# A cosine-attention and MLP kernel: the first 18 pairs of heads in another written order

## The chip, the cores and the metric

The kernel runs on one core of a Trainium2 chip. The metric is the time of one execution on the device in microseconds; for the kernel before it is the median of 3 runs. The profile comes from one further execution, which has a time of its own. The core's engines work side by side, each through its own queue in the order in which the program gives it instructions: TensorE (PE, with its weight loads shown as PEld), VectorE (DVE), ScalarE (ACT), GpSimd (POOL), and SyncE (SP), which here only starts DMAs. An instruction that waits holds up all that stands behind it in its engine's queue.

## The reference

Attention with normalised queries and keys, then an MLP on its output:

```
q_n = q / (norm(q) + 1e-6);  k_n = k / (norm(k) + 1e-6)
attn = softmax(q_n @ k_n^T / tau)          # 8 batches x 12 heads, 448 x 64, tau = 0.1
x = (attn @ v), put to 3584 x 768
h = x @ w_in                               # 768 -> 2048
g = h * clip(h + 3, 0, 6) / 6
out = g @ w_out                            # 2048 -> 768, 3584 rows
```

Inputs and output are 32-bit floats; the matrix products run in 16-bit floats.

## The kernel before

The 96 heads are 48 pairs (8 batches times 6). A pair i goes through these steps, whose names are used from here on; j is an item, a q or a k of two pairs, and a step's last letter says on which engine it runs (a is ACT, v DVE, p POOL):

- LQ.j loads a q or k item (448 KB, L197) and LV loads v (four DMAs, L211), both on SP's queue.
- SQ squares an item (L226 on ACT, L228 on DVE or POOL; some items in parts), RE sums the rows (DVE, L240), NO (or NA and ND) makes the reciprocal norms on ACT (L256 to L259), NM normalises (L296).
- TR transposes an item on PE (seven matmuls, L342); XD does it by a transposing DMA on SP (L353). CQ, CK and CS copy the result to where the scores read it: `kz` for k, `tT` for q, `km` for a rest (L362 on ACT, L364 and L392 on DVE, L402 on POOL).
- SC.i.c makes the scores of one of four parts of a pair (PE, L442 and L445), EX.i.c their exponentials on ACT (L464).
- VC casts v (L313 on DVE, L315 on POOL and ACT), VA.i.c multiplies by v on PE into PV (L487), FI divides by the row sums (DVE, L507 and L508).
- BK transposes the result on PE (L525, L527), or XP and XB by DMA (L559, L546); CX copies it into `xT`, the MLP's input.

The MLP runs in units U on PE, taken from a list in fixed order: one 128-wide slice of the first matmul (L609, called F0.0 to F0.15 for batch 0 and F1.x for batch 1), a tile of the second matmul (L682, S0), or one of the products of a scheme that multiplies 2 x 2 blocks with fewer products (L818, named 3.-1, 4.-1 and so on). UA and UV do what a unit leaves to ACT and to DVE: the relu (L629) and the product u times M that goes to `gT` (L636), or the store of a tile. UP does sums on POOL.

The scheme needs sums of blocks of `w_out`: WS.x.e.h makes half h of sum x on engine e (L762, 128 x 1536 elements). 6, 7 and 1 go to `w_sum`; y3 and y4 go back into `w_out_sb` itself. Sums of blocks of `gT` are GS (L796) and GL. W starts the next of ten loads of weights on POOL's queue (L1036; six pieces of `w_in`, then four of `w_out`).

D.n and DP.n issue n matmuls on zeros, of 512 and of 248 columns (L1043, L1048), which go nowhere: they keep PE busy while it would wait. PSUM has two score banks and the banks Y and Z until OPEN; from then on scores and units take their banks from a ring of six (M0, M1, Y, Z, M2, M3), so that a bank comes round when its readers (EX, or UA and UV) are done.

What sets the order: pairs 0 to 17 (`FIRST = 18`) follow PLAN, 38 strings of such names, written out by hand. The program goes through it from left to right and gives each engine its instructions in that sequence, so two neighbours on one engine keep their order, and two on different engines are bound only by data, buffers and banks. Each step asserts that the steps it needs stand ahead of it. Pairs 18 to 47 are issued by a loop, which is the same in both kernels. PLAN's interpreter:

```
def run(text):
    for t in text.split():
        op, *args = t.split(".")
        do(op, *(int(a) if a.lstrip("-").isdigit() else a for a in args))

for line in PLAN:
    run(line)
```

Of the kernel before, what the change touches and what calls it, by code (L numbers as in the profile page):

```python
# [18 lines left out]
ORDER = "1111111111111111111111111111112222222122"  # L19

PLAN = [
# [38 lines left out]
]  # L60


# [1164 lines left out]
```

## Time and profile before

| | us |
|---|---|
| time, median of 3 runs (lowest, highest) | 401.3 (401.23, 401.36) |
| the profiled execution | 401.5 |
| its span in the profile | 399.7 |
| PE busy | 391.1 |
| DVE busy | 291.4 |
| ACT busy | 274.1 |
| POOL busy | 235.7 |

The span runs from the first to the last instruction that the profile shows. Busy times of different engines lie side by side in it. PLAN's part ends some 120 us into the span; until 58 us there is too little for PE to do without attention, and until about 8 us the first items are on their way.

In a row of the timeline the first number is the start, the second the length, both in us, then the engine, the line, the operation, what it writes and reads, and the count of like instructions in a row; in square brackets stands the idle time ahead of it and what ended that. In a row of waits stand engine and line, what was waited for, the sum, the times, and the longest. Rows by window list busy time and count for each engine, then the granted clock (1.00 is full), the share of the DMA engines and what they moved in GB/s.

### The profile page before, as it was taken

How to read it: one execution, taken by the hardware profiler on the slowest of the kernel's cores; microseconds unless marked ns; L12 is line 12 of the kernel's file. 1: busy time of each engine (PE TensorE's matmuls, PEld its weight loads, DVE VectorE, ACT ScalarE, POOL GpSimd, SP SyncE). 2: the span in 40 equal slices, each digit the busy share in tenths (PEclk: the TensorE clock that was granted, in tenths of full speed). 3: DMA queues.
4: the chain of work that ended last, by engine and by line, in shares of the span. 5: the costliest groups of instructions: out<-in, count | busy, mean ns of one | idle time of the engine just before them, and what ended most of it. 6: DMA issues, size and time to landing. Idle time of an engine off the chain costs nothing.

```text
span 399.7 us, 9624 instructions
## 1 busy us (share of the span) xinstructions
PE 391.1 (98%) x3669; PEld 231.3 (58%) x3669; DVE 291.4 (73%) x514; ACT 274.1 (69%) x627; POOL 235.7 (59%) x234
## 2 busy tenths in 40 slices
PE   7999999999999999999999999999999999999996
PEld 5666466555565555555555555555565556555563
DVE  7797987889788688767888775976756565645663
ACT  6999999777887676887776776767658655224230
POOL 6896628552574989579769839788395500500070
PEclk9999999999999999999999999999999999999999
DMA  8999995896997778795879296884843424130123
GB/s 290 278 267 234 240 274 158 149 200 138 232 180 161 180 177 179 164 231 157 196 171 241 78 202 158 174 184 135 194 111 88 103 48 67 45 75 21 30 71 97
DMA packets 92365, 63.73 MB, mean 159 GB/s; under 512 B 56096, under 2 KB 91552, under 8 KB 92320
## 3 DMA queue, kind: packets, MB, share of 16 engines
q1 hardware_dynamic: 87408, 56.45, 58.0%
q0 software_dynamic: 4512, 6.29, 9.2%
q8 instruction: 28, 0.46, 0.5%
q10 hardware_dynamic: 400, 0.39, 0.3%
q14 instruction: 17, 0.14, 0.1%
HBM read 45.61 MB, written 11.01 MB: 142 GB/s over the span
## 4 chain that ended last, share of the span: by engine, by line
PE 92%; ACT 5%; DVE 2%; issue 0%; ACTq 0%
PE M L609 25%; PE M L818 20%; PE PV L487 11%; PE Y L609 6%; PE Z L609 6%; PE M L445 6%; PE Z L818 5%; PE Y L818 4%; ACT at L464 4%; PE PV L1048 2%; PE Y L445 1%; PE M L906 1%; PE Z L445 1%; DVE w_out_sb L762 1%; PE M L682 1%; PE Z L682 1%
## 5 line engine op out<-in xcount | busy, mean ns | idle before, releaser
L609 PE MATMUL M<-xT,w_in_sb 128*128 128x448 bf16 x516 | 109.4, 352 | 0.1
L609 PEld LDWEIGHTS <-w_in_sb 128*128 128x128 bf16 x768 | 72.1, 98 | 62.3 <-issue 1.8
L464 ACT ACTIVATE at<-M 128x448 bf16<-128x448 f32 x194 | 96.9, 568 | 14.6 <-PE M L445 13.6
L296 POOL TENSOR_TENSOR nrm<-big,nr 128x896 bf16<-128x896 f32 (+1 forms) x45 | 76.4, 1700 | 26.2 <-ACT nr L259 15.7
L228 POOL TENSOR_TENSOR big<-big 128x896 f32<-128x896 f32 (+3 forms) x41 | 62.0, 1517 | 15.5 <-DVE n L240 10.2
L636 DVE SCALAR_TENSOR_TENSOR gT<-u,M 128x448 bf16<-128x448 bf16 x75 | 45.4, 616 | 31.6 <-ACT u L629 31.2
L629 ACT ACTIVATE u<-M 128x448 bf16<-128x448 f32 x86 | 48.0, 561 | 28.4 <-PE M L609 27.0
L487 PEld LDWEIGHTS <-at 128*128 128x128 bf16 (+1 forms) x1536 | 53.5, 97 | 22.2 <-issue 13.4
L487 PE MATMUL PV<-vx,at 128*128 128x65 bf16 (+1 forms) x1536 | 62.4, 193 | 0.1
L240 DVE TENSOR_REDUCE n<-big 128x14 f32<-128x896 f32 (+1 forms) x50 | 51.6, 1041 | 5.8 <-POOL big L228 2.9
L818 PEld LDWEIGHTS <-gT 128*128 128x128 bf16 x336 | 32.5, 98 | 24.6 <-issue 1.7
L847 POOL TENSOR_TENSOR big<-big 128x384 f32<-128x384 f32 x13 | 13.5, 1035 | 53.6 <-ACT big L871 53.5
L818 PE MATMUL M<-w_out_sb,gT 128*128 128x384 bf16 x224 | 40.3, 326 | 0.9 <-DVE w_out_sb L762 0.9
L818 PEld LDWEIGHTS <-gs 128*128 128x128 bf16 x280 | 27.0, 98 | 18.5 <-issue 0.4
L402 POOL COPY km<-tT 64x128 bf16<-64x128 bf16 x34 | 12.9, 379 | 38.7 <-PE M L445 13.8
L508 DVE TENSOR_TENSOR on<-PV,rc 128x512 bf16<-128x512 f32 x48 | 33.2, 691 | 1.7
L818 PE MATMUL M<-w_sum,gs 128*128 128x384 bf16 (+1 forms) x192 | 34.2, 323 | 0.0
L464 ACT ACTIVATE at<-Y 128x448 bf16<-128x448 f32 x51 | 28.9, 566 | 6.0 <-PE Z L445 5.9
L445 PE MATMUL M<-tT,kz 64*128 64x448 bf16 (+1 forms) x171 | 31.9, 350 | 0.1
L609 PE MATMUL Y<-xT,w_in_sb 128*128 128x448 bf16 x132 | 28.7, 353 | 0.0
L464 ACT ACTIVATE at<-Z 128x448 bf16<-128x448 f32 x49 | 27.8, 568 | 0.8 <-PE M L445 0.8
L315 POOL CAST vx<-big 128x512 bf16<-128x512 f32 x37 | 24.5, 665 | 3.7 <-PE PV L487 3.3
(138 smaller groups left out, 564.8 us busy)
## 6 DMA issues: line engine op xcount, KB each, us to landing
big<-in_k_dram SPq DMA_DIRECT2D x24, 448.0 KB, 4.6
big<-in_q_dram SPq DMA_DIRECT2D x24, 448.0 KB, 4.2
out_dram<-o SPq DMA_DIRECT2D x107, 96.0 KB, 2.2
big<-in_v_dram SPq DMA_DIRECT2D x48, 128.0 KB, 3.9
big<-in_v_dram SPq DMA_DIRECT2D x48, 96.0 KB, 3.8
w_out_sb<-in_moe_w_out_dram POOLq DMA_DIRECT2D x4, 768.0 KB, 9.1
w_in_sb<-in_moe_w_in_dram POOLq DMA_DIRECT2D x4, 384.0 KB, 8.9
w_in_sb<-in_moe_w_in_dram POOLq DMA_DIRECT2D x2, 768.0 KB, 15.1
```

The source lines that it names most:

```text
L228: engines[e].tensor_tensor(out=o, in0=i, in1=i, op=ALU.mult)
L240: nc.vector.tensor_reduce(out=n2s[d % 2][:, j % 2, c], in_=sq[:, :, :, :].rearrange("p g c d -> p (g c) d")[:, c, :], axis=AX.X, op=ALU.add,)
L296: engines[e].tensor_tensor(out=nrm[:, :, g, :].rearrange("p c g d -> p g c d"), in0=raw_of[j][:, g, :, :], in1=rs[d % 2][3][:, j % 2, :] . ...
L315: (engines[e].copy if e == "a" else engines[e].tensor_copy)(out=o, in_=f)
L445: nc.tensor.matmul(o, ks, qt[rows], start=True, stop=True)
L464: nc.scalar.activation(out=o, in_=x, func=AF.Exp, scale=inv_tau)
L487: nc.tensor.matmul(pv_out(j, h), at[rows, n, q_cols(i // HP, j)], vt[rows, 3 + h if name == "M" else 5 * h + int(name[1]), :], start=(name ...
L508: nc.vector.tensor_tensor(out=on[:, :, :, :].rearrange("p j h d -> p h j d"), in0=pv4[:, :, :, 0:D], in1=rc[:, :, :].to_broadcast([128, 2, ...
L609: nc.tensor.matmul(ps[:, 0:S], w_in_sb[:, cc, fc * 128 : (fc + 1) * 128], x[:, cc, 0:S], start=(cc == 0), stop=(cc == CC - 1),)
L629: nc.scalar.activation(out=u[:, :], in_=ps[:, 0:S], func=AF.Relu, bias=0.5, scale=1.0 / 6.0)
L636: nc.vector.scalar_tensor_tensor(out=g[:, fc, c0 : c0 + S], in0=u[:, :], scalar=1.0, in1=ps[:, 0:S], op0=ALU.min, op1=ALU.mult,)
L818: nc.tensor.matmul(m, lhs[:, c, :], rhs[:, c, c0 : c0 + width], start=(base is None and c == 0), stop=(c == KC - 1), skip_group_check=True,)
```

## The change

Only the 38 strings of PLAN differ. The steps are the same but for the engine of seven and the count of dummies: CK.0, CS.6, CS.9 and CX.9 go from DVE to ACT, CQ.13 from ACT to DVE, VC.11 from POOL to DVE, VC.19 from ACT to POOL; the short dummies (DP) go from 75 to 64. All else is order. The second and third rows of PLAN, as an example:

```diff
-    "NO.0.1 LQ.5 LQ.4 LV.0 DP.5 DP.8 DP.1 DP.2 SQ.3.a.0.7 NM.1.p.0 DP.6 DP.4 D.10 SQ.0.v.6.2 RE.0.0 RE.0.1 DP.4",
-    "NM.1.v.1 NO.0.0 NM.0.p.0 SQ.2.a.0.7 RE.3 RE.2 NM.0.p.1 TR.1.Y TR.0.Z CK.0.v DP.4 SQ.4.p.0.7 CQ.0.v LQ.6",
+    "NO.0.1 LQ.5 LQ.4 LQ.6 LV.0 DP.8 DP.5 SQ.3.a.0.7 SQ.0.v.6.2 RE.0.0 RE.0.1 NM.1.v.1 NM.1.p.0 DP.4 D.10 NO.0.0",
+    "NM.0.p.0 SQ.2.a.0.7 RE.3 SQ.5.a.0.7 RE.2 NM.0.p.1 TR.1.Y SQ.4.p.0.7 DP.4 DP.2 TR.0.Z CQ.0.v CK.0.a DP.4 DP.1",
...
```

On PE the first transposes (TR.1, TR.0) stood behind 30 short, 10 long and 4 short dummies; now behind 21 short and 10 long, with 6 short ones between the two. ACT's queue at this place, before (L226 squares, L256 to L259 norms, L464 the first exps; `tT` here is the copy CQ.1):

```order
L226 ACTIVATE big<-big 128x896 x2
L256 ACTIVATE ln_106<-n_103 128x28
L257 ACTIVATE nr_107<-ln_106 128x28
L258 ACTIVATE ln_106<-nr_107 128x28
L259 ACTIVATE nr_107<-ln_106 128x28
L362 COPY tT_84<-Z 128x448
L464 ACTIVATE at_0_86<-SC_149 128x2x448
```

and now:

```order
L226 ACTIVATE big<-big 128x896 x2
L362 COPY kz_80<-Y 128x448
L256 ACTIVATE ln_106<-n_103 128x28
L257 ACTIVATE nr_107<-ln_106 128x28
L258 ACTIVATE ln_106<-nr_107 128x28
L259 ACTIVATE nr_107<-ln_106 128x28
L362 COPY tT_84<-Z 128x448
L464 ACTIVATE at_0_86<-SC_149 128x2x448
```

The copy of the first transposed k (CK.0) came in ahead of the four norm steps of the second pair of items.

DVE's queue at the weight sums, before (the first L762 is WS.y3.v.0, then WS.6.v.1, FI.13 in two rows, WS.1.v.1, WS.7.v.1, a copy that stores a tile, and three at once: y3.v.1, y4.v.0, y4.v.1; L392 is CK.15 at the top and CK.16 at the end):

```order
L392 COPY kz1_81<-tT0_83 128x384
L636 SCALAR_TENSOR_TENSOR gT1_72<-u_1594,M1_649 128x448
L762 TENSOR_TENSOR w_out_sb_68<-w_out_sb_68 128x4x384
L762 TENSOR_TENSOR w_sum6_74<-w_out_sb_68 128x1536
L507 RECIPROCAL rc_1660<-PV_109 128x8
L508 TENSOR_TENSOR on_1535<-PV_109,rc_1660 128x2x4x64
L762 TENSOR_TENSOR w_sum1_73<-w_out_sb_68 128x1536
L762 TENSOR_TENSOR w_sum7_75<-w_out_sb_68 128x1536
L695 COPY o_1666<-Z_111 128x384
L762 TENSOR_TENSOR w_out_sb_68<-w_out_sb_68 128x4x384 x3
L392 COPY kz0_80<-tT0_83 128x384
```

and now (from the last product of F1, L636):

```order
L636 SCALAR_TENSOR_TENSOR gT1_72<-u_1582,M1_667 128x448
L762 TENSOR_TENSOR w_sum7_75<-w_out_sb_68 128x1536
L762 TENSOR_TENSOR w_sum6_74<-w_out_sb_68 128x1536
L762 TENSOR_TENSOR w_out_sb_68<-w_out_sb_68 128x4x384
L507 RECIPROCAL rc_1647<-PV_109 128x8
L508 TENSOR_TENSOR on_1521<-PV_109,rc_1647 128x2x4x64
L392 COPY kz1_81<-tT0_83 128x384
L762 TENSOR_TENSOR w_sum1_73<-w_out_sb_68 128x1536
L695 COPY o_1672<-Z_111 128x384
L762 TENSOR_TENSOR w_out_sb_68<-w_out_sb_68 128x4x384 x3
L313 TENSOR_REDUCE vx1_96<-big_94 128x8x64
L392 COPY kz0_80<-tT0_83 128x384
```

CK.15 went behind three pieces and FI.13; SP's transposing DMA XD.16 follows it in PLAN and needs its buffer, and POOL's NM.19 in turn waits for XD.16. WS.7.v.1 went to the front, and the cast VC.17 (L313) came in ahead of CK.16. Farther up, WS.6.v.0 now stands ahead of the product (UV) of F1.8 instead of behind it and CK.14, and on POOL WS.1.p.0 ahead of CS.14.

SP's queue around the loads of items 13 to 18, before (the k load at the top is LQ.14; L211 rows are LV.5; the five after them LQ.13, 15, 18, 17, 16; L559 is XP.6):

```order
L197 DMA big_94<-in_k_dram 128x2x448
L211 DMA big_94<-in_v_dram 64x2x256
L211 DMA big_94<-in_v_dram 64x2x192 x2
L211 DMA big_94<-in_v_dram 64x2x256
L197 DMA big_94<-in_k_dram 128x2x448
L197 DMA big_94<-in_q_dram 128x2x448
L197 DMA big_94<-in_k_dram 128x2x448
L197 DMA big_94<-in_q_dram 128x2x448
L197 DMA big_94<-in_k_dram 128x2x448
L559 DMA_TRANSPOSE xT1_70<-on_871 128x8x128
```

and now:

```order
L211 DMA big_94<-in_v_dram 64x2x192 x2
L211 DMA big_94<-in_v_dram 64x2x256
L197 DMA big_94<-in_k_dram 128x2x448
L197 DMA big_94<-in_q_dram 128x2x448
L197 DMA big_94<-in_k_dram 128x2x448 x3
L197 DMA big_94<-in_q_dram 128x2x448
L559 DMA_TRANSPOSE xT1_70<-on_865 128x8x128
```

LQ.14 went from ahead of LV.5 to behind LQ.18: the order is now LQ.13, 15, 18, 14, 16, 17.

72 rows, old and new, of the table PLAN are left out of this document.

## The prediction

> **What bounds the kernel now.** I read the page's head first, then the waits of the matmul engine, then busy time by stage, and only then the places where the rows of PLAN differ.
>
> ```profile
> span 399.7 us, 9624 instructions
> PE 391.1 (98%) x3669; PEld 231.3 (58%) x3669; DVE 291.4 (73%) x514; ACT 274.1 (69%) x627; POOL 235.7 (59%) x234
> PE 92%; ACT 5%; DVE 2%; issue 0%; ACTq 0%
> ```
>
> PE is busy for 98% of the span and the chain that ended last runs on it for 92%. What an edit of the order can win is therefore PE's idle time, PE's own filler work, and the 5% in which the chain runs on ACT. Over the whole span PE waits at four places:
>
> ```profile
> PE PV L1048 <- DVE vx L1099: 2.5, 1, 2.5
> PE M L818 <- DVE w_out_sb L762: 0.9, 1, 0.9
> PE SC L445 <- ACT at L464: 0.3, 1, 0.3
> PE SC L442 <- ACT at L464: 0.2, 1, 0.2
> ```
>
> The first, 2.5 us, is the wait for the memsets ahead of PLAN, which do not change. The second is one stall in the weight sums. Busy time by stage (us; busy time and count of PE, PEld, DVE, ACT, POOL; granted clock; DMA share; GB/s) says what holds in between:
>
> ```profile
> 8.10:12.80 4.70, 4.64 (x40) 2.92 (x38) 3.91 (x7) 3.81 (x11) 3.84 (x5) 1.00 1.09 320
> 12.80:34.00 21.20, 20.26 (x288) 13.64 (x286) 18.56 (x40) 20.73 (x38) 16.26 (x14) 1.00 1.03 262
> 34.00:58.00 24.00, 23.80 (x302) 13.90 (x299) 20.63 (x44) 23.32 (x56) 12.44 (x14) 1.00 1.10 260
> 58.00:100.00 42.00, 41.91 (x389) 23.74 (x389) 36.31 (x62) 33.97 (x84) 24.04 (x22) 1.00 0.79 162
> ```
>
> From 12.8 to 58 ACT is the full engine (20.73 of 21.20, 23.32 of 24.00): it makes the exps (EX) that PE's value products wait for, and PE is padded with dummies. From 58 on ACT has 8 of 42 us free and PE none; a gain made before 58 then stays to the end, unless a wait eats it. Past the weight sums the two plans differ only in small ways, so I look at three places: the start, the ACT stretch, the weight sums. All clock times are those of the run before.
>
> **The start.** Here are PE, ACT, DVE and POOL around the first scores:
>
> ```profile
> 2.48 6.08 PE L1048 MATMUL PV<-xT 128*128 128x248 bf16 x30 [2.48 <-DVE vx L1099]
> 8.39 2.32 PE L1043 MATMUL Y<-xT 128*128 128x512 bf16 x10
> 10.55 0.59 PE L1048 MATMUL PV<-xT 128*128 128x248 bf16 x4
> 10.98 0.55 PE L342 MATMUL Y<-ident,nrm 128*128 128x128 bf16 x7
> 11.37 0.55 PE L342 MATMUL Z<-ident,nrm 128*128 128x128 bf16 x7
> 12.40 0.56 PE L445 MATMUL SC<-tT,kz 64*128 64x448 bf16 x4
> 8.79 1.89 ACT L226 ACTIVATE big<-big 128x896 f32<-128x896 f32 x2
> 12.38 0.53 ACT L362 COPY tT<-Z 128x448 bf16<-128x448 bf16 x1 [0.49 <-DVE tT L364]
> 12.81 0.92 ACT L464 ACTIVATE at<-SC 128x896 bf16<-128x896 f32 x1
> 7.62 1.08 DVE L296 TENSOR_TENSOR nrm<-big,nr 128x448 bf16<-128x448 f32 x1
> 11.57 0.39 DVE L364 COPY kz<-Y 128x448 bf16<-128x448 bf16 x1 [0.73 <-PE Y L342]
> 8.96 1.84 POOL L296 TENSOR_TENSOR nrm<-big,nr 128x448 bf16<-128x448 f32 x2 [0.74 <-ACT nr L259]
> ```
>
> TR.1 (10.98) has its data at 7.62 + 1.08 = 8.70 and waits only in PE's queue, behind 30 + 10 + 4 dummies. In the new plan 21 stand ahead of the ten long ones, and none between those and TR.1. Four late dummies take 10.98 − 10.55 = 0.108 us each; the thirty took 8.39 − 2.48 = 5.91, 0.197 each. If a slow one is twice 0.108, then 25 were slow and the pace changed after 25 × 0.216 = 5.4, at about 7.9. So 21 end at 2.48 + 21 × 0.216 = 7.0; the ten long ones need 10.55 − 8.39 = 2.16 at full pace, do 0.45 of it by 7.9 and end at 9.6. TR.1 then takes 0.4 to 10.0 and six dummies 0.65, so TR.0 comes at once when its POOL row ends, 8.96 + 1.84 = 10.80, and not at 11.37: −0.5. If the pace changed no sooner for the lighter load, the long ones end at 7.0 + 4.3 = 11.3 and nothing is won; if faster, TR.0 still waits for POOL. So −0.6 to +0.3, and I take −0.5. CK.0 moves to ACT, which is free from 10.68 to the copy at 12.38 but for the four short norm steps; their reader on POOL stands behind a square that now comes ahead, so 0.4 of delay there is covered. If that cover fails, the third pair is late by 0.4 and not the first. CQ.0 then has DVE for itself, SC.0.0 comes at 11.9 and the first exp at 12.3, not 12.81.
>
> **The ACT stretch.**
>
> ```profile
> L362 ACT COPY kz<-M 64x64 bf16<-64x64 bf16 x2 | 0.4, 200 | 0.0
> 34.00:58.00 24.00, 0.85 (x5) 0.42 (x5) 1.00 1.10 260
> 56.04 0.59 PE L1048 MATMUL PV<-xT 128*128 128x248 bf16 x4
> 58.10 1.29 PE M L609 x6
> ```
>
> (the second row is the dummies alone). CS.6 and CS.9 move from DVE to ACT: two copies each, 4 × 0.20 = +0.8 on the full engine. CX.9 also moves to ACT and CQ.13 off it, but beyond 58. VC.11 moves from POOL to DVE, hidden: DVE has 3.4 us free in this stage. The five dummies go; the four at 56.04 stand among value products right ahead of the first-matmul units at 58.10, worth 4 × 0.108 = 0.43, the other 0.1. ACT's idle time here is 0.47 + 0.68 = 1.15 by busy time, which is a floor since records overlap (12.38 + 0.53 is past 12.81); by starts I count 2.5. Loads are put in another order and exps moved next to their scores (EX.6.0 now before SC.6.1), which can close it. If no idle goes and the PE dummies were cover only, 58.10 moves by −0.5 + 0.8 = +0.3; if all goes, by −0.5 + 0.8 − 2.5 = −2.2. I take copies and closed idle as equal, and the dummies as won: −0.5 − 0.5 = −1.0, near the middle of the two ends.
>
> **The weight sums.**
>
> ```profile
> 95.66 1.82 DVE L762 TENSOR_TENSOR w_sum<-w_out_sb 128x1536 bf16<-128x1536 bf16 x2
> 97.86 4.18 DVE L762 TENSOR_TENSOR w_out_sb<-w_out_sb 128x1536 bf16<-128x1536 bf16 x3
> 99.18 2.05 POOL L296 TENSOR_TENSOR nrm<-big,nr 128x896 bf16<-128x896 f32 x1 [5.96 <-DMA tT<-nrm]
> 102.10 0.81 PE L818 MATMUL M<-w_out_sb,gT 128*128 128x384 bf16 x4 [0.92 <-DVE w_out_sb L762]
> 82.56 3.10 POOL L762 TENSOR_TENSOR w_sum<-w_out_sb 128x1536 bf16<-128x1536 bf16 x1
> 85.63 0.95 DVE L762 TENSOR_TENSOR w_sum<-w_out_sb 128x1536 bf16<-128x1536 bf16 x1
> 96.39 1.25 SPq L353 DMA_TRANSPOSE tT<-nrm  x1
> ```
>
> A piece takes 1.82 / 2 = 0.91 alone. Three took 4.18, so the last (y4.v.1, from 99.6) took about 2.4: it ended 0.8 after POOL's NM.19 did (101.23). PE's 0.92 at 102.10 is that. NM.19 starts when the transpose issued at 96.39 (XD.16) has landed. In the new plan XD.16 waits for CK.15, which now stands behind three pieces and FI.13; I place its issue at 97.0 and NM.19 at 99.75. The pieces of DVE stand closer; y4.v.1 comes at about 99.9 with VC.17 behind it. So NM.19 is still first, by 0.15: y4.v.1 ends at 99.75 + 2.05 + 0.8 = 102.6. PE has SC.15.3 (0.35) to do first, so it loses 0.5 − 0.35 = 0.15, and another 0.2 where SC.16.0 waits for CK.16 behind VC.17: about +0.4 against before. If NM.19 comes after, the wait goes: −0.9. WS.6.v.0 now stands ahead of UV of F1.8, and POOL's WS.1.p.0 ahead of CS.14, at about 81.9 to 85.0; if the piece waits for it, that product ends near 86.5, when U of F1.11 wants its bank: 0 to +0.3, taken as 0.
>
> The Trainium skill ("SBUF — State Buffer", section "Who interferes with whom") states that a DVE instruction with two SBUF inputs contends with a GpSimd one that reads SBUF, and the one issued first keeps the other out for its whole length. The trace agrees: 101.23 + 0.91 = 102.14, against an end at 97.86 + 4.18 = 102.04. It speaks against the change at WS.6.v.0: by it that piece, some 84 by DVE's queue, waits out WS.1.p.0, U of F1.11 loses the 0.3, and the sum below would be −0.3 and 401.0; the rows of before have DVE's piece at 85.63 just as POOL's ends (85.66), but behind another copy, so they show no wait there.
>
> **Loads.**
>
> ```profile
> 31.34 0.37 SPq L197 DMA_DIRECT2D big<-in_k_dram  x1
> 49.01 0.37 SPq L197 DMA_DIRECT2D big<-in_k_dram  x1
> big<-in_k_dram SPq DMA_DIRECT2D x2, 448.0 KB, 8.5
> 57.91 1.68 POOL L228 TENSOR_TENSOR big<-big 128x896 f32<-128x896 f32 x1 [7.92 <-DVE n L240]
> 59.55 1.70 POOL L296 TENSOR_TENSOR nrm<-big,nr 128x896 bf16<-128x896 f32 x1
> 61.98 0.55 PE L342 MATMUL M<-ident,nrm 128*128 128x128 bf16 x7
> ```
>
> LQ.14 leaves at 31.34 before; now it stands behind LQ.18, which left at 49.01. Its chain is square 1.68, NM.13 1.70, then TR.13 (61.98, or 61.0 after the gain). So it must land by 61.0 − 3.4 = 57.6. Issued at 48.5 (0.5 after LQ.18, 1.0 gained), with the 8.5 of its neighbours, it lands at 57.0: no cost, 0.6 to spare. The others on SP leave earlier or have more room; weight loads on POOL's queue move by one place, with the units that read them behind 58.
>
> **Sum.** −1.0 + 0.4 = −0.6. The profiled run took 401.5 (span 399.7 and 1.8 around it), so 400.9 there, and 400.7 against the median of 401.3.
>
> **The rivals.** A is the forecast above: 400.7, and 399.9 to 401.4 by itself (the wait at F1.11 lies in that range).
>
> B, the collision goes. For it: only 0.15 us decides who is first. Against: the transpose's issue also moves with DVE. −1.0 − 0.9 = −1.9: 399.4.
>
> C, slower: LQ.14 lands late. At 260 GB/s (the stage's row) a 448 KB load takes 1.7; one place further back in a full queue PE waits 57.0 + 1.7 − 57.6 = 1.1, two places 2.8; with 1.9 the time is 402.6. It decides from a landing 9.1 us after issue. For it: DMA share 1.10 there. Against: LQ.14 no longer loads that stretch earlier.
>
> D, the plan does not do what it says: ACT stays full, the copies eat the start's gain, +0.3 at 58.10, and with the collision's 0.4 the time is 402.0.
>
> **How the numbers follow.** 0.2% is 0.8 us, about what a measurement of this kernel tells from no change. A 0.42 (faster 0.17, same 0.24, slower 0.01), B 0.30 (0.29, 0.01, 0), C 0.14 (0, 0.02, 0.12), D 0.14 (0.02, 0.05, 0.07): faster 0.48, same 0.32, slower 0.20. The range takes in B and its neighbourhood and D with half of C: 399.0 to 402.5.
>
> **What would show it.** The first exp at 12.3; the first-matmul unit of 58.10 at 57.1; the wait of PE on w_out_sb at 0.9 to 1.1 (B: absent); no wait of PE at TR.13 (C). I am wrong if ACT shows no less idle time before 58, if the slow pace of the first dummies lasts past 8, or if a bank is not free at F1.11.

## The result and the profile after

The changed kernel took 403.93 us in the median of 20 executions (402.14 to 408.22), the kernel before 401.27 (400.76 to 404.29); by the comparison the ratio is 1.0062, 95% interval 1.0039 to 1.0085. (The ratio compares all executions of the two kernels and is not the quotient of the two medians.) It is slower, and above the range that was given, 399.0 to 402.5. Two things are in that: the lowest time rose by 1.4 us, and the spread grew from 3.5 to 6.1 us. The profiled execution is one of the shorter ones: 402.71, its span 400.9, 1.2 above the 399.7 of before. So the profile shows the first part, and further profiles are needed for the second.

Head of the page, then all waits of PE (columns as before: sum, times, longest):

```profile
span 400.9 us, 9597 instructions
PE 389.9 (97%) x3658; PEld 230.4 (57%) x3658; DVE 294.4 (73%) x510; ACT 275.0 (69%) x631; POOL 237.7 (59%) x234
PE 82%; DVE 6%; DMA 4%; ACT 3%; POOL 1%; SPq 1%; issue 1%; DVEq 0%; ACTq 0%; POOLq 0%
```

```profile
PE PV L1048 <- DVE vx L1099: 2.5, 1, 2.5
PE M L818 <- DVE w_out_sb L762: 1.1, 1, 1.1
PE Z L342 <- POOL nrm L296: 0.8, 1, 0.8
PE SC L442 <- ACT at L464: 0.7, 2, 0.4
PE M L609 <- DMA xT<-on: 0.6, 1, 0.6
PE Y L342 <- POOL nrm L296: 0.5, 1, 0.5
PE PV L487 <- DVE on L508: 0.4, 2, 0.2
```

The chain lost ten points of PE to DVE, DMA and POOL. Where four waits stood there are seven, and two of the new ones (the wait for xT, and the one for Y at L342) go back to a load or a transpose that was issued later than before. The rows around them, in the timeline of the new plan: the start (PE, ACT), then TR.6 (POOL, PE), CS.6 on ACT, the value products where the dummies at 56.04 had stood (PE), the last unit of the ACT stretch (F0.8), the weight sums (POOL, DVE, PE), and the end of PLAN (PE, SP):

```profile
6.64 2.32 PE L1043 MATMUL Y<-xT 128*128 128x512 bf16 x10
8.91 0.55 PE L342 MATMUL Y<-ident,nrm 128*128 128x128 bf16 x7
10.92 0.56 PE L342 MATMUL Z<-ident,nrm 128*128 128x128 bf16 x7 [0.83 <-POOL nrm L296]
12.39 2.54 ACT L464 ACTIVATE at<-SC 128x896 bf16<-128x896 f32 x3
24.36 1.68 POOL L228 TENSOR_TENSOR big<-big 128x896 f32<-128x896 f32 x1 [1.76 <-DMA big<-in_k_dram]
26.00 1.70 POOL L296 TENSOR_TENSOR nrm<-big,nr 128x896 bf16<-128x896 f32 x1
27.75 0.56 PE L342 MATMUL Y<-ident,nrm 128*128 128x128 bf16 x7 [0.53 <-POOL nrm L296]
34.48 0.44 ACT L362 COPY kz<-Z 64x64 bf16<-64x64 bf16 x2
55.58 0.40 PE L487 MATMUL PV<-vx,at 128*128 128x65 bf16 x8 [0.20 <-DVE on L508]
58.39 0.92 PE L609 MATMUL M<-xT,w_in_sb 128*128 128x448 bf16 x4
100.06 1.80 POOL L296 TENSOR_TENSOR nrm<-big,nr 128x896 bf16<-128x896 f32 x1 [6.48 <-DMA tT<-nrm]
98.49 4.18 DVE L762 TENSOR_TENSOR w_out_sb<-w_out_sb 128x1536 bf16<-128x1536 bf16 x3
102.72 0.81 PE L818 MATMUL M<-w_out_sb,gT 128*128 128x384 bf16 x4 [1.07 <-DVE w_out_sb L762]
124.12 0.35 PE L609 MATMUL M<-xT,w_in_sb 128*128 128x448 bf16 x1 [0.61 <-DMA xT<-on]
117.25 2.46 SPq L667 DMA_DIRECT2D out_dram<-o  x4
119.76 3.58 SPq L546 DMA_TRANSPOSE xT<-on  x2
```

Following one step after another through both traces gives the account of the 1.2 us (new less old start of the same step on PE). The first exp is 0.42 earlier, as forecast. At TR.6 the sign turns: POOL stood idle 1.76 us for LQ.9, which landed at 24.2 instead of 21.3, so NM.6 and TR.6 came late; −0.43 became +0.16. Between 34 and 38 another 0.15 is lost: CS.6 on ACT (the 0.44 at 34.48) puts EX.6.0 back. F0.8 stands at 58.39, +0.3. In the weight sums DVE's pieces and POOL's NM.19 collide as before, and that costs another 0.28: +0.56. At 124 PE waits for a transposed xT: XB.16, issued behind the four stores at 117.25 instead of ahead of them: +0.8. That makes +1.3, and 0.1 of it comes back behind PLAN: +1.2.

### The profile page after: what moved, and what is told of

It reads as the page before. It is cut to its first block, busy times and chain, and to the rows that moved or that the text cites. A ratio compares the mean times of both kernels' runs of the same rounds, so it can differ in the third digit from the quotient of the medians.

```text
span 400.9 us, 9597 instructions
## 1 busy us (share of the span) xinstructions
PE 389.9 (97%) x3658; PEld 230.4 (57%) x3658; DVE 294.4 (73%) x510; ACT 275.0 (69%) x631; POOL 237.7 (59%) x234
## 4 chain that ended last, share of the span: by engine, by line
PE 82%; DVE 6%; DMA 4%; ACT 3%; POOL 1%; SPq 1%; issue 1%; DVEq 0%; ACTq 0%; POOLq 0%
PE M L609 23%; PE M L818 19%; PE PV L487 10%; PE Y L609 6%; PE Z L818 5%; PE Z L609 5%; PE M L445 5%; PE Y L818 4%; DMA big<-in_k_dram 2%; ACT at L464 2%; PE Y L445 1%; PE M L906 1%; DVE w_out_sb L762 1%; DMA xT<-on 1%; DVE w_sum L762 1%; PE Z L445 1%
## 5 line engine op out<-in xcount | busy, mean ns | idle before, releaser
L464 ACT ACTIVATE at<-M 128x448 bf16<-128x448 f32 x195 | 97.4, 568 | 15.2 <-PE M L445 14.1
L636 DVE SCALAR_TENSOR_TENSOR gT<-u,M 128x448 bf16<-128x448 bf16 x75 | 45.3, 615 | 27.5 <-ACT u L629 27.3
L818 PE MATMUL M<-w_out_sb,gT 128*128 128x384 bf16 x216 | 39.2, 326 | 1.1 <-DVE w_out_sb L762 1.1
L402 POOL COPY km<-tT 64x128 bf16<-64x128 bf16 x34 | 14.6, 429 | 35.5 <-PE M L445 10.1
L464 ACT ACTIVATE at<-Y 128x448 bf16<-128x448 f32 x52 | 29.5, 568 | 6.0 <-PE Z L445 5.9
L464 ACT ACTIVATE at<-Z 128x448 bf16<-128x448 f32 x47 | 26.8, 569 | 1.6 <-PE M L445 1.6
```

The lines of the kernel that those rows point to most:

```text
L464: nc.scalar.activation(out=o, in_=x, func=AF.Exp, scale=inv_tau)
L636: nc.vector.scalar_tensor_tensor(out=g[:, fc, c0 : c0 + S], in0=u[:, :], scalar=1.0, in1=ps[:, 0:S], op0=ALU.min, op1=ALU.mult,)
L818: nc.tensor.matmul(m, lhs[:, c, :], rhs[:, c, c0 : c0 + width], start=(base is None and c == 0), stop=(c == KC - 1), skip_group_check=True,)
```

## The experiments

The theory after this profile (L): transfers issued later make the loss, LQ.9 at TR.6, XB.16 at 124, and LQ.14 in executions in which it lands later than here. Its rivals: the copies moved to ACT, the weight sums, or something at the start. Each edit is to PLAN alone. "Before" in each case is the kernel before, run on the same chip at the same time.

### Each late transfer put back

LQ.9 ahead of LV.2 and LQ.10 again:

```diff
-DP.4 LV.2 LQ.10 LQ.9 SC.1.2.0
+DP.4 LQ.9 LV.2 LQ.10 SC.1.2.0
```

> The new plan with one load back in its old place: LQ.9 ahead of LV.2 and LQ.10 on SP's queue instead of behind them. Theory L (late loads make the loss): in the new plan LQ.9 landed at 24.2 instead of 21.3, POOL stood idle 1.76 us for it ahead of SQ.9, NM.6 came late and TR.6 made PE wait 0.53 at 27.75; with LQ.9 early that wait goes, the unit F0.8 comes at about 57.8 instead of 58.39, and the time falls by about 0.6 against the new plan. Rival R (ACT is full there and the moved copies are what costs): the wait may go, but F0.8 stays at 58.3 to 58.4 and the time stays.

Measured: 403.22 in the median (401.17 to 406.02), before 401.33; ratio 1.0032, interval 1.0007 to 1.0057. In its profile the wait at TR.6 is gone and F0.8 stands 0.32 ahead of before, 0.62 ahead of the new plan. So L holds for this place and the rival falls. The profile shows something else beside it, in POOL's and DVE's rows at the weight sums:

```profile
99.54 2.49 POOL L296 TENSOR_TENSOR nrm<-big,nr 128x896 bf16<-128x896 f32 x1 [6.66 <-DMA tT<-nrm]
97.79 2.69 DVE L762 TENSOR_TENSOR w_out_sb<-w_out_sb 128x1536 bf16<-128x1536 bf16 x3
```

NM.19 starts 1.75 after the three pieces (1.57 in the new plan) and now POOL takes 2.49 and DVE 2.69: the last piece got in first, and PE's 1.1 us wait is absent. 0.18 us decided it. All 20 profiles of this case fit that: the third piece is due 1.73 after the first; in 13 NM.19 started 1.32 to 1.58 after the first piece and the three took 4.18 or 4.19, in seven it started 1.75 or later and they took 2.69.

LQ.14 back ahead of LV.5:

```diff
-CS.10.v U LV.5
+CS.10.v LQ.14 U LV.5
...
-LQ.18 LQ.14 LQ.16
+LQ.18 LQ.16
```

> The new plan with LQ.14 back ahead of LV.5 on SP's queue (some 14 us earlier). Theory L: in the profiled run of the new plan LQ.14 landed at 58.14 and TR.13 had only 0.67 us to spare, so runs in which it lands later make PE wait there, and that is why the new plan's times reach from 402.1 to 408.2; with LQ.14 early the times draw together, median near 402.7, spread within 1.5 us. Rival S (the scatter is not from this load): median stays near 403.9 and single runs still reach 405 and more.

Measured: 403.11 (402.32 to 405.66); ratio 1.0051, interval 1.0025 to 1.0076. The lowest did not fall, the highest fell from 408.2 to 405.7 and not to 404. Neither expectation fits well, and the interval overlaps that of the new plan, so whether this load takes any part of the spread can't be told from this run. Its three executions above 405 have a mean clock of 0.993 to 0.996, the rest at least 0.998; what that means is shown further down.

XB.16 back ahead of the stores:

```diff
-CK.18.v UV UV U
+CK.18.v XB.16 UV UV U
...
-RE.22 XB.16 EX.17.3
+RE.22 EX.17.3
```

> The new plan with the transposing DMA XB.16 back ahead of the last products' stores on SP's queue. Theory L: PE's wait of 0.61 us at 124.12 for xT goes and the time falls by about 0.6 against the new plan. Rival R: the wait at 124 is cover for another one behind it, and the time stays.

Measured: 402.50 (401.43 to 404.08); ratio 1.0019, interval 0.9999 to 1.0040. The wait at 124 is gone, one of 0.17 for the transpose after it (125.05) is there, and the lowest time fell by 0.7. L holds for the wait. The profiled execution gained less: its span is 400.6 against 400.9, as PE had come 0.24 later at 117 already and lost 0.33 at 125. Over all profiles, six of nine with XB.16 behind the stores show the wait for it (0.5 to 1.0), and none of eleven with it ahead.

All three together:

> All three back (LQ.9, LQ.14, XB.16), the rest of the new plan as it is. Theory L: the three terms add up: the 402.7 of the new plan's profiled run less 0.6 and 0.6 gives 401.4 to 401.6, with little scatter, about the time of the kernel before. Rival R: at least 402.3, since what was lost lies in the copies moved to ACT and in the weight sums.

Measured: 402.07 (401.36 to 404.69), the profiled one 401.73; ratio 1.0004, interval 0.9983 to 1.0026. The profiled time is near what L said, and all but one execution lie within 1.4 us. The medians do not add up: the single edits lowered them by 0.7, 0.8 and 1.4, the three together by 1.9.

### A longer execution of the new plan

The new plan unchanged, in one more execution with a profile.

> The new plan unchanged, profiled once more, because its executions reach from 402.1 to 408.2 and the profile shown is one of 402.7. Theory X (XB.16 and the other late transfers: the same waits grow): in a slower execution PE's wait for xT at about 124 is longer than 0.6 us, by about what the run is longer. Theory L14: the wait for NM.13 at TR.13 (62.3) appears, which the profile shown did not have. Rival: PE's waits are the same and the time lies elsewhere.

It took 405.23 (one execution, span 403.4), and the rival comes nearest: the time is lost elsewhere, at the very start. Its rows there (ACT, PE), and the stretches with the granted clock (the third figure from the end):

```profile
8.75 0.95 ACT L226 ACTIVATE big<-big 128x896 f32<-128x896 f32 x1 [1.62 <-DMA big<-in_k_dram]
12.53 0.93 PE L342 MATMUL Z<-ident,nrm 128*128 128x128 bf16 x7 [2.56 <-POOL nrm L296]
```

```profile
10.00:12.50 2.50, 0.00 (x0) 0.00 (x0) 1.90 (x2) 2.44 (x6) 1.84 (x2) 0.89 1.07 282
12.50:15.00 2.50, 2.48 (x16) 1.45 (x16) 1.52 (x4) 1.49 (x6) 1.51 (x1) 0.50 0.59 167
15.00:17.50 2.50, 2.50 (x22) 1.44 (x21) 2.47 (x3) 2.45 (x3) 2.50 (x3) 0.92 0.93 233
```

LQ.3, issued at 1.76 as in the profile above, landed at 8.66 and not at 6.67. ACT's square of item 3 stands ahead of the norms of item 0 in ACT's queue, so those, NM.0 and TR.0 came late by as much. PE had run out of dummies: it idled for 2.56 us, and from 11.97 on its clock was granted at 0.50 for 3.41 us, so that SC.0.0 came 2.4 later than in the profile above. The waits at 124 (0.6) and at the weight sums (1.1) are the same in both. So there is a fourth cause, at the start.

### The parts alone, on the kernel before

The new start in the old kernel:

```diff
-    "NO.0.1 LQ.5 LQ.4 LV.0 DP.5 DP.8 DP.1 DP.2 SQ.3.a.0.7 NM.1.p.0 DP.6 DP.4 D.10 SQ.0.v.6.2 RE.0.0 RE.0.1 DP.4",
-    "NM.1.v.1 NO.0.0 NM.0.p.0 SQ.2.a.0.7 RE.3 RE.2 NM.0.p.1 TR.1.Y TR.0.Z CK.0.v DP.4 SQ.4.p.0.7 CQ.0.v LQ.6",
-    "SQ.5.a.0.7 LQ.7 SC.0.0.0 NO.1 NM.3.p LV.1 CK.1.v RE.5 CQ.1.a RE.4 SC.0.1.1 EX.0.0 DP.3 DP.3 DP.3 SC.0.2.0 EX.0.1",
+    "NO.0.1 LQ.5 LQ.4 LV.0 DP.5 DP.8 SQ.3.a.0.7 NM.1.p.0 DP.4 D.10 SQ.0.v.6.2 RE.0.0 RE.0.1",
+    "NM.1.v.1 NO.0.0 NM.0.p.0 SQ.2.a.0.7 RE.3 SQ.5.a.0.7 RE.2 NM.0.p.1 TR.1.Y DP.4 DP.2 TR.0.Z CQ.0.v CK.0.a DP.4 DP.1 SQ.4.p.0.7 LQ.6",
+    "LQ.7 NO.1 NM.3.p LV.1 CK.1.v RE.5 CQ.1.a SC.0.0.0 RE.4 SC.0.1.1 EX.0.0 DP.3 DP.3 DP.3 SC.0.2.0 EX.0.1",
```

> The kernel before with the new start alone: 21 short dummies ahead of the ten long ones, six between TR.1 and TR.0, CK.0 on ACT; loads and all else in the old order. If the start's gain carries to the end (theory of the prediction, first part): first exp 0.43 to 0.5 earlier, F0.8 at 57.6 to 57.7, time about 400.9. If ACT or PE eats it (rival D): F0.8 at 58.1, time 401.3.

Measured: 401.69 (401.24 to 404.82), before 401.43; ratio 1.0017, interval 1.0000 to 1.0034. Its lowest is 0.5 above the lowest of before: no gain. The profile fell on the longest execution (LQ.3 late again, PE idle 2.07 ahead of TR.0, clock 0.70 from 15 to 20), so where the gain went in a quiet execution, one without a late load, is not shown, and this stays open.

XP.12 ahead of XD.16 in the old kernel, so that NM.19 comes later:

```diff
-SC.15.0 XD.16 EX.14.2 FI.13 XP.12
+SC.15.0 EX.14.2 FI.13 XP.12 XD.16
```

> The kernel before with XP.12 ahead of XD.16 on SP's queue, nothing else: XD.16 leaves 1.3 us later, so NM.19 starts after y4.v.1 has begun. Theory K (who starts first decides the collision): the last of the three L762 pieces takes 0.9 and not 2.4, PE's wait of 0.9 at 102.1 goes, the time falls by 0.9 to about 400.4. Rival: the late transpose costs as much behind CK.16 and SC.16, time 401.3 or more.

Measured: 402.06 (400.70 to 403.94); ratio 1.0016, interval 0.9998 to 1.0035. From its profile (DVE, POOL, PE):

```profile
99.48 2.69 DVE L762 TENSOR_TENSOR w_out_sb<-w_out_sb 128x1536 bf16<-128x1536 bf16 x3
110.22 0.61 POOL L315 CAST vx<-big 128x512 bf16<-128x512 f32 x1 [1.72 <-DMA big<-in_v_dram]
113.51 1.46 PE L818 MATMUL Z<-w_sum,gs 128*128 128x384 bf16 x8 [1.06 <-DVE big L881]
```

The three pieces take 2.69 and PE's wait on them is gone (its steps come 1.08 sooner against the step ahead of it): K holds. But ten microseconds on PE waits 1.06. VC.18 on POOL waits for LV.9, with the sums of the products behind it, whose bank PE needs; and LV.9 came no sooner. It landed at 110.07, against 108.20 before, in an execution that had run 1.6 later ever since its start (LQ.3 had landed at 8.24). VC.18 had waited 0.40 in the kernel before and now waited 1.72, and the whole gain was given back there. The new plan has VC.18 behind those sums; the next kernel has that order too, and PE does not wait there.

### The parts together

The new plan with the three transfers back and this swap:

```diff
-CK.15.v XD.16 WS.1.v.1 XP.12 LQ.22
+CK.15.v WS.1.v.1 XP.12 XD.16 LQ.22
```

> The new plan with LQ.9, LQ.14 and XB.16 back in place and XP.12 ahead of XD.16. If the parts add up: a_three's profiled 401.7 (median 402.1) less 1.1 for PE's wait on the weight sums and up to 0.3 behind it gives 400.4 profiled and a median near 400.8, below the kernel before. Rival: another wait takes the place and the time stays at 401.5 or more.

Measured: 401.03 (400.37 to 401.27), before 401.43; ratio 0.9975, interval 0.9959 to 0.9992. Its profile has a span of 398.7 and no wait on the weight sums, and none behind. To see if that low spread was luck:

> The new plan with the three loads back and XP.12 ahead of XD.16, measured once more on another occasion. If its low spread (400.4 to 401.3) was a matter of luck at the start, which it shares with the new plan, some executions now reach 402 and more; the lowest stays at 400.4 and the fast ones at 400.4 to 401.3. If the spread is the new plan's late transfers, all stay under 401.5.

Measured on another occasion: 401.12 (400.45 to 404.42), before 401.39; ratio 0.9998, interval 0.9973 to 1.0022. Two of the twelve were 404 with a mean clock of 0.995: luck, then, as the first expectation said, and the other ten reach to 401.73. The medians are 0.4 and 0.3 below the kernel before, but the second interval holds 1: a version beyond the kernel before is likely and not proven.

### The start: a load issued late, and the dummies

LQ.2 issued ahead of LQ.3, in the new plan and in the old:

```diff
-SQ.0.a.0.6 LQ.3 LQ.2
+SQ.0.a.0.6 LQ.2 LQ.3
```

> The new plan with LQ.2 issued ahead of LQ.3, so that LQ.3 lands about 1.2 us later (7.9 instead of 6.7): a late load made on purpose. Theory S: ACT's square of item 3 starts 0.7 to 0.8 later, NO.0.0 behind it and TR.0 too; TR.0 comes at 11.6 to 11.7 instead of 10.92, PE's idle time ahead of it grows from 0.83 to about 1.6, and all of the 0.7 to 0.8 reaches the first exp, more if the clock falls. Rival: dummies and later slack take it up, the first exp moves by under 0.3.

> The kernel before with the same late load (LQ.2 ahead of LQ.3). Theory S: its TR.0 stood at 11.37 behind dummies with its data at 10.80, so 0.57 of the delay is covered: TR.0 at 11.5 to 11.7, PE's idle time ahead of it at most 0.3, clock 1.00, first exp 0.15 to 0.3 later. Rival: it is as sensitive as the new plan, first exp 0.7 or more later.

The new plan: 406.52 (four executions, 404.31 to 408.82; ratio 1.0125, interval 1.0079 to 1.0171). The old one: 402.01 (401.58 to 404.92; ratio 1.0015, interval 0.9995 to 1.0036). PE's row in the new plan:

```profile
11.69 0.56 PE L342 MATMUL Z<-ident,nrm 128*128 128x128 bf16 x7 [1.21 <-POOL nrm L296]
```

LQ.3 landed at 7.83, 1.16 later than in the new plan's first profile; TR.0 and all behind it came 0.77 later, to 84 us, and that at full clock; the distance then grew to 1.2 at 117 and 1.6 at 124, where the wait for xT was 1.0 and not 0.6. Two of the four executions (408.6 and 408.8) have a mean clock of 0.99. Theory S holds for the new plan. For the old one the profile fell on an execution with LQ.3 at 9.83, long past its cover too (PE idle 2.82, clock 0.60 to 0.72), so its 0.15 to 0.3 can't be read there; by medians it lost 0.6 where the new plan lost 2.6, the latter from four executions only. That the old start covers a late LQ.3 at least in part can be read in the profile of the swap above: it landed 1.60 later than in the kernel before, and TR.0 came 0.73 later (12.10).

The dummies back, in the new plan:

```diff
-NM.1.p.0 DP.4 D.10 NO.0.0
+NM.1.p.0 DP.9 DP.4 D.10 DP.4 NO.0.0
```

> The new plan with the dummies of the start as before: 30 short and 4 more around the ten long ones ahead of TR.1 (nine and four added). Theory S (the thin start passes on every late load): in a slow execution of the new plan LQ.3 landed at 8.66 instead of 6.67, PE stood idle 2.56 us ahead of TR.0 and ran at granted clock 0.50 after it. With the dummies back PE is busy until 11, the clock stays at 1.00, and the times draw together: highest below 406, median under 403.5; a quiet execution is at most 0.5 slower than the new plan's 402.3. Rival (the scatter is elsewhere): the spread stays 402 to 408.

Measured: 403.66 (402.76 to 406.49); ratio 1.0057, interval 1.0033 to 1.0081. The clock part came out: no execution below 0.998. Over all runs, of 129 executions with the thin start (21 dummies) 17 have a mean clock below 0.9975; of 143 of the kernel before and its swap, 4; of 25 with the dummies put back, none. But the spread stayed, with executions of 404 to 406.5 at full clock: S explains only a part of it.

> The new plan with the old amount of dummies at the start, profiled again: its executions reach 402.8 to 406.5 with the clock at 1.00, so what makes the long ones is not the clock. Theory X: in an execution above 404 PE's wait for xT (XB.16) at about 123 is 1 us or more longer than the 0.6 of the profile at hand. Theory L14: PE waits for NM.13 at TR.13. Rival: the whole start is later by what the run is longer, LQ.3 having landed late, with the clock at 1.00. In an execution near 402.8 none of it is there.

This profile and two more of the same kernel took 403.54, 402.24 and 403.23. None is above 404, so the long ones were not caught. The first shows a wait for NM.13 at TR.13 of 0.2 (LQ.14 landed at 59.11), as L14 says, and the 0.6 at 124. In the third TR.0 came 1.1 later than in the new plan's first profile with no wait of PE ahead of it: there the dummies themselves held it up, as PE's slow pace at the start lasted longer (to 8.2; 6.5 there).

The version with the parts together, and the dummies back too:

> The new plan with the three loads back, XP.12 ahead of XD.16, and the old amount of dummies ahead of TR.1: lowest 400.4 as without the dummies, and none of its executions with the clock below 0.997; median 400.5 to 401.2, below the kernel before. Rival: the dummies cost the start's gain back and the median is 401.3 or more.

Measured: 401.64 (400.55 to 402.48), before 401.18; ratio 0.9994, interval 0.9976 to 1.0012. No clock loss, as expected, but the median is that of the rival. The average of its executions (401.52) is that of the repeat without the dummies (401.56), so in these two the dummies cost about what they insure; the first run without them averaged 400.87.

### One late load each, put into the version without any

> As the version with the three loads back and XP.12 ahead of XD.16 (400.4 to 401.7 with the clock at 1.00, medians 401.03 and 401.12), but LQ.14 left where the new plan has it. Theory L14: in executions in which it lands after 58.7 PE waits at TR.13 (0.34 in one execution with a landing at 59.11), so the lowest stays at 400.4 and the median rises by 0.3 to 1.0. Rival: LQ.14 had its slack back and median and spread do not change.

Measured: 402.05 (400.33 to 405.02), before 401.29; ratio 1.0013, interval 0.9993 to 1.0032. Without the late load it was 401.03 and 401.12 on other occasions. Lowest and median are as L14 said; its wait did not show. LQ.14 landed at 56.92 and there is no wait at TR.13. Its profile, DVE, POOL and PE:

```profile
44.76 1.60 DVE L283 TENSOR_SCALAR ln<-nr 128x28 f32<-128x28 f32 x1 [0.21 <-ACT nr L272]
45.15 1.72 POOL L315 CAST vx<-big 128x512 bf16<-128x512 f32 x3
47.26 0.35 PE L445 MATMUL M<-tT,kz 128*128 128x448 bf16 x1 [1.16 <-DVE gT L636]
```

and the same place where LQ.9 alone is late, the next kernel:

```profile
44.63 0.37 DVE L283 TENSOR_SCALAR ln<-nr 128x28 f32<-128x28 f32 x1 [0.22 <-ACT nr L272]
45.02 0.63 POOL L315 CAST vx<-big 128x512 bf16<-128x512 f32 x1
46.80 1.18 POOL L315 CAST vx<-big 128x512 bf16<-128x512 f32 x2 [1.15 <-PE PV L487]
```

With LQ.14 out of the way LV.5 lands earlier (44.45, against 46.65), so VC.9 and the two casts behind it run on POOL as one train instead of one and two (the last row names PE, but LV.5 landed only 0.15 ahead of that start). A small DVE instruction (ND.5, L283) that began 0.39 before the train took 1.60 instead of 0.37; the product behind it was late, its bank too, and PE waited 1.16. In the first profile of the new plan the train is there as well (three casts in 1.73 from 45.43), hits NM.10 instead (1.94 us, not 1.08), and PE does not wait. Over the profiles of the new plan and its variants the train is in all ten with LQ.14 late and in one of six with it early (the repeat of the parts together). In ten of these eleven ND.5 takes 0.37, NM.10 takes 1.93 or 1.94 (five) or 1.38 to 1.41 (five), and PE does not wait. So the wait of 1.16 is shown in one execution; that it makes the median of 402.05, or the long executions at full clock, is not shown.

> As the version with the three loads back and XP.12 ahead of XD.16, but LQ.9 left behind LV.2 and LQ.10 as in the new plan. Theory L: PE waits at TR.6 for NM.6 in most executions, 0.55 to 0.62 later at F0.8, median 401.6 to 401.8. Rival: the later gain takes it up, median 401.1.

Measured: 401.10 (400.04 to 403.47); ratio 0.9996, interval 0.9978 to 1.0013. LQ.9 landed at 23.81, PE waited 0.15 at TR.6, and the median did not change: the rival. So LQ.9's price changes from one execution to the next: of ten profiles with it late, six show a wait of 0.15 to 0.73 at TR.6; the first profile's 0.53 is nearer the upper end. On this occasion the version with only LQ.14 late lay 1.0 above this one.

## Why the prediction was wrong, point by point

- The start: right in the quiet profile, the first one of the new plan. TR.0 at 10.92, first exp at 12.39 (forecast 10.8 and 12.3). The pace of the dummies changed at 6.5 and not at 7.9; as the step said for that case, TR.0 still waited for POOL (0.83). The step said what happens if the pace of the dummies changes later, but not what happens if a load is late: the 0.57 us by which TR.0's data had been early was counted as waste to be won, and it was cover for LQ.3. This is where a part of the spread comes from.
- The ACT stretch, "I take copies and closed idle as equal, and the dummies as won": wrong. CS.6 cost 0.15, and the dummies at 56.04 were cover only: PE now waits there for FI.8 (0.20, the row at 55.58), and the distance to before is 0.3 at 55 and at 58.4. The end "if the PE dummies were cover only: +0.3" is the one that came, though by another sum: −0.43 + 0.59 + 0.15.
- Loads, "The others on SP leave earlier or have more room": this failed first. LQ.9 leaves 1.6 later, behind LV.2 and LQ.10, and landed 2.9 later; POOL's square was waiting for it, and PE lost 0.6. I had followed one load of the queue, LQ.14, and not the others.
- LQ.14: it landed at 58.14 and not at 57.0, but the limit had moved too, to 58.8, as everything ran later; no cost in that profile, as forecast. Rival C's wait showed in one of the later ones with 0.2. What I missed is what its absence does: the loads behind it come sooner and POOL's casts bunch, which held DVE and then PE in one execution (1.16). The median is about 1.0 higher with LQ.14 late (402.05 against 401.10 on the same occasion); what makes that 1.0 stays open.
- The weight sums: right in kind and size. A and not B, a wait of 1.07, and 0.28 lost (forecast 0.4). XD.16 left at 97.30 (97.0), NM.19 started at 100.06 (99.75). WS.6.v.0 cost nothing at F1.11 in the quiet profile, as taken; in other executions PE lost 0.1 to 0.3 there.
- "Past the weight sums the two plans differ only in small ways": wrong. XB.16 went behind four stores on SP, and PE waited for it (0.61); the distance to before grew by 0.8.
- Sum: forecast −0.6; the quiet profile shows +1.2. The 1.8 between the two are LQ.9 with 0.6, XB.16 with 0.8 and the dummies that were not won with 0.5, with small ones that cancel. The +0.3 at F0.8 and the 0.28 at the weight sums are close to rival D's figures, but that is luck: LQ.9 made the +0.3, and D's copies had only 0.15 of it. The other 1.2 to the median of 403.93 lies in executions longer than that profile; the thin start is shown for some of them, the rest is open.
- What the edits give back: with the three transfers in their old places the median falls by 1.9, to 402.07, which the interval does not tell from the kernel before. Parting NM.19 from the sums takes another 1.0 (402.07 to 401.03), but the kernel before has that collision too, so most of this is a gain of its own and not what the change lost (0.28 in the quiet profile). How the 1.9 divides among LQ.9, LQ.14 and XB.16 is not shown, as the single edits do not add up to it.

## What to carry to other kernels

When an order is searched against fixed landing times, the slack that it removes was the cover for the spread of those times: ask of every wait that you close what the data ahead of it does when it comes 1 or 2 us late, and judge by many executions and not by one profile. When you move one transfer, go through every transfer behind it too, the ones that come earlier as well as those that come later, and ask what their users will run into. A gain at one place is kept only as far as the next shared queue lets it.

## What the runs showed of the hardware

- The third load of the program, issued at 1.75 or 1.76 us, landed at 6.6 to 7.8 us in most and at 8.2 to 8.8 in four, with the same two loads ahead of it.
- With the first matmul at 2.48 us in every profile, the full clock was granted from a time between 5.2 and 8.5 us on.
- Ahead of TR.0 idle times of PE of 2.07, 2.56 and 2.82 us came with 3.41 us at a granted clock of 0.50 each, which began between 0.6 before and 1.9 after the end of the idle time; idle times of 1.17 and 1.21 did not. The Trainium skill ("TensorE: Matmul & The Clock Gate", section "What's actually happening") gives about 3.4 us of idle time for that; the runs here show it with less.
- DVE's and POOL's instructions held each other up whole in these places. An 0.37 us instruction of 28 elements a partition took 1.60 beside three casts; three L762 pieces took 2.69 with NM.19 starting 1.75 after them and 4.18 with 1.57.
